# Feature-map attention and two MoE blocks on one core: weights' exponents rebased by ScalarE, a square kept in PSUM, the first loads from SP

## The chip, the cores and the metric

One core of a Trainium2 chip runs the whole program. The metric is device time in microseconds of one execution. Three runs of the kernel before took 1725.16, 1725.84 and 1729.33 us (median 1725.84). TensorE (PE in the rows, PEld for its weight loads), VectorE (DVE), ScalarE (ACT), GpSimd (POOL) and the queue engine SyncE (SP) each work through their own instructions in order.

## The reference

```python
def phi(x):                                  # x: (8, 8, 576, 64)
    proj = einsum('bhsd,df->bhsf', x, w_phi)             # 64 -> 128
    proj = proj - max(abs(proj), axis=-1, keepdims=True)
    return concatenate([exp(proj), exp(-proj)], axis=-1)
q_p, k_p = phi(q), phi(k)
kv = einsum('bhsf,bhsd->bhfd', k_p, v)
z = sum(k_p, axis=2)
x = einsum('bhsf,bhfd->bhsd', q_p, kv) / (einsum('bhsf,bhf->bhs', q_p, z)[..., None] + 1e-06)
x = x.transpose(0, 2, 1, 3).reshape(4608, 512)
h = x @ w_in                                 # moe1: 512 -> 2048
x = (h - tanh(h)) @ w_out                    # 2048 -> 512
a, b = x @ w1, x @ w2                        # moe2: 512 -> 1024
out = (a * b @ w3) @ w_out2                  # 1024 -> 1024 -> 512
```

The MoE weights arrive as 64-bit floats and are turned into 32-bit ones on the chip; each is then used as a high and a low part, with three products (hh, lh, hl) for one.

## The kernel before, in words

**Attention** works on 32 steps of one pair of batches and one head, in tiles of 128 rows, nine to a step. The tiles are taken in slots of four (`G`), so nine slots make four steps. In a slot TensorE projects k and, a step later, q of the slot's tiles (`p_pe`), turns the q differences of the slot before (`t_pe`), adds up kv (`kv_pe`) and, in eight slots of nine, makes one half of an output (`o_pe`); in some it also sums z (`z_pe`) and turns kv (`kv_turn`). VectorE takes maximum and difference of every p (L227, L229) and copies kv and half of the outputs out of PSUM; ScalarE takes the exponentials; GpSimd sums k's features. An output goes from PSUM to a buffer `st` and from there in six stores by SP to DRAM. p has three PSUM banks (`ps_h`), which moe1's h uses later.

**Weight chunks** run beside it, 26 of 128x512 in attention (tiles `craw`, `ct`), 92 of 128x256 in moe1 (`eraw`, `et`). `conv_steps` reads the two 32-bit words of each 64-bit float: ScalarE takes Abs of the high word read as a float (L117), VectorE takes a maximum with 2^-15 (L121), shifts left by 3 and masks (L124), and sets the sign and top bit from the raw word (L127); ScalarE scales the low word (L132), GpSimd adds the two (L135), ScalarE rounds to the high part (L139) and GpSimd subtracts for the low part (L142, or L607 elsewhere).

**moe1** goes through 9 blocks of 512 rows times 16 chunks of w_in, 144 n. Each n has twelve products into h (`mm1`) and twelve into four y banks (`mm2`), which lags by two n. Between them stands `act_g`: u = h^2 and tanh on ScalarE (L515, L516), s = (u + C1)^2 and the mask m (L517, L518), h - tanh (L522), then on VectorE u = h C2 u (L523), u = (s + C0) u (L525) and a predicated copy for small h (L526). In `act_g(n)`, after m, the g of n - 1 is split: gh on ScalarE (L541), gl on GpSimd (L542). SBUF pools of moe1 lie where attention's lay, so the first write to a tile there waits for the last user of that place, stores from `st` included. The next block's x is loaded, multiplied by the reciprocal (L1029) and split (L1035, L1036) in between.

**moe2** follows with all its products in TensorE's order; the first two `w34` products are mixed with moe1's last `mm2`.

Order is set by the code: each engine executes what it is given in the order in which the loops call it.

Of the kernel before, what the change touches and what calls it, by code (L numbers as in the profile page):

```python
# [8 lines left out]
F32 = mybir.dt.float32  # L9
# [3 lines left out]
ACTF = mybir.ActivationFunctionType  # L13
ALU = mybir.AluOpType
# [24 lines left out]
CW = S // 2  # L39
CE = S // 4  # L40
# [5 lines left out]
C0 = 4.726447630264936  # L46


TINY = 2.0 ** -15
FC_EARLY = 13  # L50


# [1 line left out]
def kernel(ctx, tc, qk_in, v_in, w_phi, w_in, w_out, w12, w3t_in, wo2, out):  # L54
    nc = tc.nc
    PE, ACT, DVE, POOL, SP = nc.tensor, nc.scalar, nc.vector, nc.gpsimd, nc.sync
    PSUM = bass.MemoryType.PSUM
# [45 lines left out]
    def words(raw, dt=U32):  # L103
        r = raw.bitcast(dt).rearrange("p (n two) -> p n two", two=2)
        return r[:, :, 0], r[:, :, 1]

    def conv_steps(pool, pre, n, load, dst, nb=1, nraw=None):

        o = {}

        def s_load():
            o["raw"] = pool.tile([128, n], I64, tag=f"{pre}raw", name=f"{pre}raw", bufs=nraw)
            load(o["raw"])

        def s_abs():
            o["t"] = pool.tile([128, n], U32, tag=f"{pre}t", name=f"{pre}t", bufs=nb)
            ACT.activation(o["t"].bitcast(F32), words(o["raw"], F32)[1], ACTF.Abs)  # L117

        def s_max():
            t = o["t"].bitcast(F32)  # L120
            DVE.tensor_scalar(t, t, TINY, None, ALU.max)  # L121

        def s_shift():
            DVE.tensor_scalar(o["t"], o["t"], 3, 0x3FFFFFF8, ALU.logical_shift_left, ALU.bitwise_and)  # L124

        def s_a():
            DVE.scalar_tensor_tensor(o["t"], words(o["raw"])[1], 0xC0000000, o["t"], ALU.bitwise_and, ALU.bitwise_or)  # L127

        def s_c():

            o["c"] = words(o["raw"])[0]
            ACT.activation(o["c"], words(o["raw"])[0], ACTF.Copy, scale=2.0 ** -29)  # L132

        def s_add():
            POOL.tensor_tensor(o["t"], o["t"], o["c"], ALU.add)  # L135

        def s_hi():
            o["hi"], o["lo"] = dst()
            ACT.activation(o["hi"], o["t"].bitcast(F32), ACTF.Copy)  # L139

        def s_lo():
            POOL.tensor_tensor(o["lo"], o["t"].bitcast(F32), o["hi"].bitcast(F32), ALU.subtract)  # L142

        on_act.update((s_abs, s_c, s_hi))
        return [s_load], [s_abs], [s_max, s_shift], [s_c, s_a], [s_add], [s_hi], [s_lo], lambda: o["t"].bitcast(F32)

    def fc_view(t):
        return t.rearrange("p k f -> p (k f)")

    def w_in_chunk(pool, i, part=0, of=1, pre="c", nb=1, nraw=None):  # L150
        nk = NK // of
        c = slice(part * nk * 128, (part + 1) * nk * 128)

        def dst():
            if part == 0:
                slots["in", i] = two("wi", i, [NK, 128])
            return tuple(fc_view(t[:, part * nk:(part + 1) * nk]) for t in slots["in", i])

        return conv_steps(pool, pre, DM // of, lambda raw: SP.dma_start(raw, w_in[i][:, c]), dst, nb, nraw)

    def w_out_chunk(pool, i, part=0, of=1, pre="c", nb=1, nraw=None):
        c = slice(part * DM // of, (part + 1) * DM // of)

        def dst():
            if part == 0:
                slots["out", i] = two("wo", i, [DM])
            return tuple(t[:, c] for t in slots["out", i])

        return conv_steps(pool, pre, DM // of, lambda raw: SP.dma_start(raw, w_out[i * 128:(i + 1) * 128, c]), dst, nb, nraw)
# [2 lines left out]

    def attention():
        with ExitStack() as es:
            pool = es.enter_context(tc.tile_pool(name="att", bufs=2))
            one = es.enter_context(tc.tile_pool(name="att1", bufs=1))
            ps_t = es.enter_context(tc.tile_pool(name="ps_t", bufs=1, space=PSUM))
# [13 lines left out]

            qk, vv = {}, {}

            def load_step(st):
                t = qk[st] = pool.tile([128, PT], F32, tag="qk", name="qk")
                if st == 0:
                    for c in (slice(0, 512), slice(512, PT)):
                        SP.dma_start(t[64:, c], qk_in[st][64:, c])
                elif st == NPAIR:
                    ACT.dma_start(t[:64], qk_in[st][:64])  # L200
                else:
                    ACT.dma_start(t, qk_in[st])

            def load_v(st):
                if st < NPAIR:
                    vv[st] = pool.tile([128, TPP + 1, D], F32, tag="v", name="v", bufs=3)
                    ACT.dma_start(vv[st], v_in[st])

            pq, pk, dq, dk, kp, pt, qp = {}, {}, {}, {}, {}, {}, {}

# [160 lines left out]

            def o_out(st, c, ps):
                bp, h = divmod(st - 1, H)
                t = pool.tile([128, CW + CE], F32, tag="st", name="st")
                if c:
                    DVE.tensor_copy(t, ps[:, :CW + CE])
                else:
                    ACT.activation(t, ps[:, :CW + CE], ACTF.Copy)
                for b in range(2):
                    c0 = bp * PT + b * S + c * CW  # L380
                    SP.dma_start(num_d[h * D:(h + 1) * D, c0:c0 + CW], t[b * D:(b + 1) * D, :CW])
                    for e in range(2):
                        r = 64 * b + 32 * e
                        SP.dma_start(den_d[bp, h:h + 1, c0 - bp * PT + e * CE:c0 - bp * PT + (e + 1) * CE], t[r:r + 1, CW:])
                return bp if c and h == H - 1 else None
# [25 lines left out]
            for i in (1, 0):  # L411
                SP.dma_start(wphi[i * D:(i + 1) * D], w_phi)
            for st in range(2):
                load_step(st)
                load_v(st)
            DVE.memset(ones, 1.0)
            o_at = {}
            for st in range(1, n_steps):
# [6 lines left out]
            for s in range(n_end):  # L425
# [40 lines left out]
                for n in tiles_of(s - 1) if ok(s - 1) else ():  # L466
                    st, t = where(n)
                    if t == TPP - 1 and st + 2 < n_steps:
                        load_v(st + 2)
                for n in tiles_of(s) if ok(s) else ():  # L470
                    st, t = where(n)
# [28 lines left out]
    def moe1():  # L500
        with ExitStack() as es:
            p1 = es.enter_context(tc.tile_pool(name="m1", bufs=1))
            p2 = es.enter_context(tc.tile_pool(name="m2", bufs=2))
            p3 = es.enter_context(tc.tile_pool(name="m3", bufs=2))
            ps_y = es.enter_context(tc.tile_pool(name="ps_y", bufs=1, space=PSUM))

            gg, yy, tt = {}, {}, {}

            def act_g(n, ys):
                h = hh[n]  # L510
                u = p2.tile([128, 512], F32, tag="u", name="u")
                s = p1.tile([128, 512], F32, tag="s", name="s")
                t = p2.tile([128, 512], F32, tag="t", name="t")
                m = p1.tile([128, 512], F32, tag="m", name="m")
                ACT.activation(u, h, ACTF.Square)  # L515
                ACT.activation(t, h, ACTF.Tanh)  # L516
                ACT.activation(s, u, ACTF.Square, bias=c1_sb)  # L517
                ACT.activation(m, u, ACTF.Relu, bias=lim_sb, scale=-1.0)  # L518
                g_parts(n - 1)
                for d in range(3):  # L520
                    y_out(ys, d)
                DVE.tensor_tensor(t, h, t, ALU.subtract)  # L522
                DVE.scalar_tensor_tensor(u, h, C2, u, ALU.mult, ALU.mult)  # L523
                y_out(ys, 3)
                DVE.scalar_tensor_tensor(u, s, C0, u, ALU.add, ALU.mult)  # L525
                DVE.copy_predicated(t, m.bitcast(U32), u)  # L526

                x = extra.get(n, [])
                for f in x:
                    if f in on_act:  # L530
                        f()
                del hh[n]
                tt[n] = t

            def g_parts(n):
                if n < 0:
                    return
                t = tt.pop(n)
                gh = p3.tile([128, 512], F32R, tag="gh", name="gh")
                gl = p3.tile([128, 512], F32R, tag="gl", name="gl")  # L540
                ACT.activation(gh, t, ACTF.Copy)  # L541
                POOL.tensor_tensor(gl, t, gh.bitcast(F32), ALU.subtract)  # L542
                gg[n] = gh, gl

            def y_out(ys, d):
                if ys is None:
                    return
                j, pss = ys
                if d == 3 and j == NB - 1:
                    t = p2.tile([128, 512], F32, tag="t", name="t")  # L550
                else:
                    t = p1.tile([128, 512], F32, tag="yo", name="yo", bufs=3)
                if d < 3:
                    ACT.activation(t, pss[d], ACTF.Copy)
                else:
                    DVE.tensor_copy(t, pss[d])
                (ACT if d < 3 else SP).dma_start(y_d[d * 128:(d + 1) * 128, j * 512:(j + 1) * 512], t)
# [117 lines left out]
            for i in range(FC_EARLY, NFC):  # L675
                for f in (w_in_chunk, w_out_chunk):
                    for part in range(2):
                        c = f(p2, i, part, 2, "e", 5, 3)
# [8 lines left out]
            for n in range(n_all + LAG):  # L687
# [5 lines left out]
                if n == n_all:  # L693
                    g_parts(n - 1)
# [398 lines left out]
```

## Time and profile before

| | before |
|---|---|
| median of 3 runs | 1725.84 us |
| the profiled execution's own time | 1728.21 us |
| its span, first to last instruction | 1726.4 us |
| TensorE busy (modelled ends) | 1693.6 us, 98% |
| VectorE, ScalarE, GpSimd busy | 1352.1, 926.0, 1014.1 us |
| mean granted TensorE clock | 0.998 |

The profile is of one execution. Busy time is the sum of an engine's instructions; an instruction that waits for a resource after it has started counts as busy. The span has three stages: attention to 351 us, moe1 to about 1149, then moe2, in which TensorE and its weight loads are busy without a gap.

### The profile page before, as it was taken

How to read it: one execution, taken by the hardware profiler on the slowest of the kernel's cores; microseconds unless marked ns; L12 is line 12 of the kernel's file. 1: busy time of each engine (PE TensorE's matmuls, PEld its weight loads, DVE VectorE, ACT ScalarE, POOL GpSimd, SP SyncE). 2: the span in 40 equal slices, each digit the busy share in tenths (PEclk: the TensorE clock that was granted, in tenths of full speed). 3: DMA queues.
4: the chain of work that ended last, by engine and by line, in shares of the span. 5: the costliest groups of instructions: out<-in, count | busy, mean ns of one | idle time of the engine just before them, and what ended most of it. 6: DMA issues, size and time to landing. Idle time of an engine off the chain costs nothing.

```text
span 1726.4 us, 30481 instructions
## 1 busy us (share of the span) xinstructions
PE 1693.6 (98%) x10640; PEld 1436.0 (83%) x10640; DVE 1352.1 (78%) x1910; ACT 926.0 (54%) x1881; POOL 1014.1 (59%) x966
## 2 busy tenths in 40 slices
PE   7999999999999999999999999999999999999999
PEld 5666666668877888878888788888999999999999
DVE  6999999769887888888999897755757666666664
ACT  4666676557666666767777676534322232322221
POOL 5787888737576767675767575234525253535341
PEclk9999999999999999999999999999999999999999
DMA  5555555322223332333434332728988898889885
GB/s 165 158 162 164 179 176 176 96 75 76 83 95 116 110 133 93 117 106 120 126 116 125 116 111 89 263 64 294 320 283 296 282 297 278 301 274 305 277 265 197
DMA packets 173113, 305.57 MB, mean 177 GB/s; under 512 B 21728, under 2 KB 57952, under 8 KB 172960
## 3 DMA queue, kind: packets, MB, share of 16 engines
q1 hardware_dynamic: 159920, 267.48, 47.6%
q10 hardware_dynamic: 13040, 36.15, 6.6%
q8 instruction: 84, 1.38, 0.3%
q14 instruction: 69, 0.57, 0.1%
HBM read 240.34 MB, written 63.21 MB: 176 GB/s over the span
## 4 chain that ended last, share of the span: by engine, by line
PE 72%; DVE 15%; DMA 5%; ACT 2%; POOL 2%; issue 2%; SPq 2%; DVEq 0%; ACTq 0%; POOLq 0%
PE h L495 16%; PE y L571 15%; PE q L826 14%; PE q L835 7%; PE pa L826 6%; PE o L835 3%; DVE u L525 3%; PE h L733 3%; DVE t L526 2%; PE p L220 2%; PE kv L298 2%; PE o L355 2%; DVE m L227 2%; DVE et L124 1%; DMA num_d<-st 1%
## 5 line engine op out<-in xcount | busy, mean ns | idle before, releaser
L542 POOL TENSOR_TENSOR gl<-t,gh 128x512 fp32r<-128x512 f32 x144 | 201.7, 1401 | 177.2 <-ACT gh L541 118.5
L571 PE MATMUL y<-gh,w 128*128 128x512 f32 x936 | 237.4, 391 | 4.4 <-ACT gh L541 2.7
L826 PE MATMUL q<-w,w 128*128 128x384 f32 x1152 | 215.1, 334 | 0.0
L571 PEld LDWEIGHTS y<-gh,w 128*128 128x128 f32 x936 | 176.0, 188 | 42.4 <-ACT gh L541 3.4
L525 DVE SCALAR_TENSOR_TENSOR u<-s,u 128x512 f32<-128x512 f32 x144 | 202.3, 1405 | 4.7
L826 PEld LDWEIGHTS q<-w,w 128*128 128x128 f32 x1152 | 201.0, 188 | 0.0
L897 POOL TENSOR_TENSOR xa<-c,c 128x384 f32<-128x384 f32 x48 | 51.9, 1082 | 249.8 <-DVE c L896 179.3
L495 PE MATMUL h<-xa,w 128*128 128x512 f32 x780 | 188.2, 391 | 0.0
L515 ACT ACTIVATE u<-h 128x512 f32<-128x512 f32 x144 | 85.8, 596 | 183.5 <-PE h L495 177.0
L495 PEld LDWEIGHTS h<-xa,w 128*128 128x128 f32 x780 | 147.2, 189 | 31.2 <-issue 0.2
L526 DVE COPY_PREDICATED t<-m,u 128x512 f32<-128x512 uint32 x144 | 165.7, 1151 | 5.0
L876 ACT ACTIVATE c<-pa 128x384 f32<-128x384 f32 x48 | 23.6, 493 | 237.5 <-PE pa L826 190.9
L495 PE MATMUL h<-xb,w 128*128 128x512 f32 x624 | 150.0, 389 | 0.0
L571 PE MATMUL y<-gl,w 128*128 128x512 f32 x468 | 132.6, 396 | 6.9 <-POOL gl L542 6.7
L495 PEld LDWEIGHTS h<-xb,w 128*128 128x128 f32 x624 | 117.1, 188 | 24.5
L135 POOL TENSOR_TENSOR et<-et,eraw 128x256 uint32<-128x256 uint32 x92 | 68.8, 748 | 111.9 <-ACT u L515 35.8
L240 ACT ACTIVATE kp<-dk 128x512 f32<-128x512 f32 x144 | 83.0, 627 | 86.5 <-DVE dk L229 80.6
L522 DVE TENSOR_TENSOR t<-h,t 128x512 f32<-128x512 f32 x144 | 98.3, 683 | 39.5 <-ACT t L516 39.4
L523 DVE SCALAR_TENSOR_TENSOR u<-h,u 128x512 f32<-128x512 f32 x144 | 98.6, 685 | 34.0 <-ACT m L518 33.7
L227 DVE TENSOR_REDUCE m<-p 128x4 f32<-128x512 f32 (+1 forms) x145 | 98.4, 679 | 28.6 <-PE p L220 28.4
L835 PE MATMUL q<-w,w 128*128 128x384 f32 x612 | 112.8, 334 | 0.0
L571 PEld LDWEIGHTS y<-gl,w 128*128 128x128 f32 x468 | 87.4, 189 | 30.5 <-POOL gl L542 12.8
(156 smaller groups left out, 3870.1 us busy)
## 6 DMA issues: line engine op xcount, KB each, us to landing
w<-w_d SPq DMA_DIRECT2D x504, 256.0 KB
w_d<-w SPq DMA_DIRECT2D x84, 256.0 KB
qk<-in_qk ACTq DMA_DIRECT2D x31, 576.0 KB
v<-in_v ACTq DMA_DIRECT2D x32, 320.0 KB
num_d<-st SPq DMA_DIRECT2D x128, 72.0 KB
xn<-num_d SPq DMA_DIRECT2D x36, 256.0 KB
xb<-y_d SPq DMA_DIRECT2D x24, 384.0 KB
eraw<-in_w SPq DMA_DIRECT2D x32, 256.0 KB
```

Source lines behind the costliest of these rows:

```text
L227: DVE.tensor_reduce(m[:, :n], what[g][:, j], AX.X, ALU.max, apply_absolute_value=True)
L240: ACT.activation(kp[g][:, sgn, span(js)], dk[g][:, span(js)], ACTF.Exp, scale=1.0 - 2 * sgn)
L495: PE.matmul(ps, a[:, kk, :], b[kk], start=m == 0, stop=m == 3 * NK - 1)
L515: ACT.activation(u, h, ACTF.Square)
L522: DVE.tensor_tensor(t, h, t, ALU.subtract)
L523: DVE.scalar_tensor_tensor(u, h, C2, u, ALU.mult, ALU.mult)
L525: DVE.scalar_tensor_tensor(u, s, C0, u, ALU.add, ALU.mult)
L526: DVE.copy_predicated(t, m.bitcast(U32), u)
L542: POOL.tensor_tensor(gl, t, gh.bitcast(F32), ALU.subtract)
L571: PE.matmul(yy[j][d], w[:, d * 128:(d + 1) * 128], x, start=i == 0 and m == 0, stop=i == NFC - 1 and m == 2,)
L826: PE.matmul(ps, w[:, a, c], x[b][:, kk, :], start=start and m == 0, stop=m == 5, skip_group_check=True)
L835: PE.matmul(ps, w[:, a, c], x[:, b, :], start=start and kk == 0 and n == 0, stop=kk == 3 and n == 2, skip_group_check=True,)
```

## The change

The Abs of the weights' high word gets a scale of 2^-112, which moves the exponent to where the shift by 3 leaves nothing to clamp or mask; the maximum goes, and the shift has one operation. `st` gets a pool of its own, opened before attention's others. The first two steps' loads go through SP's queue. s is allotted in PSUM, in a bank that nothing used in moe1. The g of n = 0 is split at the end of `act_g(0)`.

```diff
-TINY = 2.0 ** -15
+REBASE = 2.0 ** -112
@@ conv_steps
-            ACT.activation(o["t"].bitcast(F32), words(o["raw"], F32)[1], ACTF.Abs)
-
-        def s_max():
-            t = o["t"].bitcast(F32)
-            DVE.tensor_scalar(t, t, TINY, None, ALU.max)
+            ACT.activation(o["t"].bitcast(F32), words(o["raw"], F32)[1], ACTF.Abs, scale=REBASE)
 
         def s_shift():
-            DVE.tensor_scalar(o["t"], o["t"], 3, 0x3FFFFFF8, ALU.logical_shift_left, ALU.bitwise_and)
+            DVE.tensor_scalar(o["t"], o["t"], 3, None, ALU.logical_shift_left)
 
         def s_a():
-            DVE.scalar_tensor_tensor(o["t"], words(o["raw"])[1], 0xC0000000, o["t"], ALU.bitwise_and, ALU.bitwise_or)
+            DVE.scalar_tensor_tensor(o["t"], words(o["raw"])[1], 0x80000000, o["t"], ALU.bitwise_and, ALU.bitwise_or)
...
-        return [s_load], [s_abs], [s_max, s_shift], [s_c, s_a], [s_add], [s_hi], [s_lo], lambda: o["t"].bitcast(F32)
+        return [s_load], [s_abs], [s_shift], [s_c, s_a], [s_add], [s_hi], [s_lo], lambda: o["t"].bitcast(F32)
@@ attention
+            outs = es.enter_context(tc.tile_pool(name="att0", bufs=2))
             pool = es.enter_context(tc.tile_pool(name="att", bufs=2))
...
-            def load_step(st):
+            def load_step(st, eng=ACT):
...
-                t = pool.tile([128, CW + CE], F32, tag="st", name="st")
+                t = outs.tile([128, CW + CE], F32, tag="st", name="st")
...
             for st in range(2):
-                load_step(st)
-                load_v(st)
+                load_step(st, SP)
+                load_v(st, SP)
@@ moe1
+            ps_g = es.enter_context(tc.tile_pool(name="ps_g", bufs=1, space=PSUM))
...
-                s = p1.tile([128, 512], F32, tag="s", name="s")
+                s = ps_g.tile([128, 512], F32, tag="s", name="s")
...
                 tt[n] = t
+                if n == 0:
+                    g_parts(0)
 
             def g_parts(n):
-                if n < 0:
+                if n not in tt:
                     return
```

In the changed program's rows line numbers differ by up to 4; the names stay.

On SP the program begins with these rows; `craw` are the weight chunks. Before:

```order
L412 DMA wphi<-in_w_phi 64x128 x2
L198 DMA qk<-in_qk 64x512
L198 DMA qk<-in_qk 64x640
L159 DMA craw<-in_w_in 128x512
L169 DMA craw<-in_w_out 128x512
```

And now:

```order
L409 DMA wphi<-in_w_phi 64x128 x2
L195 DMA qk<-in_qk 64x512
L195 DMA qk<-in_qk 64x640
L204 DMA v<-in_v 128x640
L199 DMA qk<-in_qk 128x1152
L204 DMA v<-in_v 128x640
L155 DMA craw<-in_w_in 128x512
L165 DMA craw<-in_w_out 128x512
```

Three loads have come in from ScalarE's queue, where they were the first instructions behind the table load, and stand ahead of the first chunks.

On VectorE a chunk (`ct`) stands between the maxima and differences of two slots. Before:

```order
L229 TENSOR_TENSOR dq<-p,m 128x512
L121 TENSOR_SCALAR ct<-ct 128x512
L124 TENSOR_SCALAR ct<-ct 128x512
L227 TENSOR_REDUCE m<-p 128x4
L229 TENSOR_TENSOR dk<-p,m 128x512
```

And now:

```order
L226 TENSOR_TENSOR dq<-p,m 128x512
L120 TENSOR_SCALAR ct<-ct 128x512
L224 TENSOR_REDUCE m<-p 128x4
L226 TENSOR_TENSOR dk<-p,m 128x512
```

One instruction of 128x512 has gone at each of 26 such places, and one of 128x256 at 92 places in moe1.

On ScalarE, where moe1 begins (the brackets name what an instruction waits for: PE, DVE, Activation, Pool, or a DMA semaphore). Before:

```order
L515 ACTIVATE u<-h 128x512 [waits DMAHW2_49,DMAHW3_49,DMAHW1_49,DMAHW4_49,DMAHW0_49,DMAHW5_49,DVE_49,DMAHW6_49,PE_49,DMAHW7_49,Activation_49,Pool_49]
L516 ACTIVATE t<-h 128x512
L517 ACTIVATE s<-u,cs 128x512 [waits Activation_49]
L518 ACTIVATE m<-u,cs 128x512
L515 ACTIVATE u<-h 128x512 [waits PE_49]
L516 ACTIVATE t<-h 128x512
L517 ACTIVATE s<-u,cs 128x512 [waits DVE_49,Activation_49]
L518 ACTIVATE m<-u,cs 128x512 [waits DVE_49]
L541 ACTIVATE gh<-t 128x512
```

And now:

```order
L513 ACTIVATE u<-h 128x512 [waits PE_49,DVE_49,Activation_49,Pool_49]
L514 ACTIVATE t<-h 128x512
L515 ACTIVATE s<-u,cs 128x512 [waits DVE_49,Activation_49]
L516 ACTIVATE m<-u,cs 128x512
L541 ACTIVATE gh<-t 128x512 [waits DVE_49]
L513 ACTIVATE u<-h 128x512 [waits PE_49]
L514 ACTIVATE t<-h 128x512
L515 ACTIVATE s<-u,cs 128x512 [waits Activation_49]
L516 ACTIVATE m<-u,cs 128x512
```

The first u no longer waits for any DMA, and gh of n = 0 has moved from behind the second m to behind the first, where it waits for VectorE.

## Rows read from the trace of the kernel before

**Rows 1.** Chain of waits, 322 to 331 us: start us, us, what.

```profile
322.23 1.45 PE kv L298 x12
...
325.27 0.22 PE kv L332 x8
...
326.58 0.59 PE tr L261 x4
327.17 0.33 PE kv L341 x3
327.50 1.01 PE kv L298 x8
328.51 0.97 PE o L355 x8
329.48 0.63 PE o L364 x16
330.11 1.09 PE p L220 x16
```

**Rows 2.** Six windows of nine slots, summed: us, busy of PE, PEld, DVE, ACT, POOL.

```profile
sum 250.58, PE 244.70 PEld 165.98 DVE 230.95 ACT 167.17 POOL 207.55; mean PE 40.78 PEld 27.66 DVE 38.49 ACT 27.86 POOL 34.59
```

**Rows 3.** Chain of waits, the first pieces of the program.

```profile
1.99 6.00 DMA qk<-in_qk
...
8.12 5.60 PE p L220 x29
```

**Rows 4.** Window 2 to 8 us: busy per engine, clock, DMA share, GB/s.

```profile
2.00:8.00 6.00, 0.00 (x0) 0.00 (x0) 0.00 (x0) 0.22 (x2) 0.00 (x0) 1.00 0.96 286
```

**Rows 5.** Groups by line, VectorE, attention: xcount | busy us, mean ns | idle before.

```profile
L124 DVE TENSOR_SCALAR ct<-ct 128x512 uint32<-128x512 uint32 x26 | 22.8, 877 | 0.9
L121 DVE TENSOR_SCALAR ct<-ct 128x512 f32<-128x512 f32 x26 | 20.2, 777 | 0.0
```

**Rows 6.** Chain of waits where moe1 begins.

```profile
355.44 1.14 DMA den_d<-st
...
356.68 0.60 ACT u L515
...
363.96 4.15 PE y L571 x10
368.10 2.73 PE h L495 x12
```

**Rows 7.** Timeline, TensorE: moe1's first products, and the first of w34.

```profile
351.40 8.48 PE L495 MATMUL h<-xa,w 128*128 128x512 f32 x36
...
1149.23 5.60 PE L733 MATMUL h<-w 128*128 128x512 f32 x24
```

**Rows 8.** Windows of 2 us behind TensorE's two longest gaps; the clock follows the counts.

```profile
364.00:366.00 2.00, 2.00 (x6) 1.56 (x7) 1.97 (x2) 1.25 (x2) 1.59 (x1) 0.58 0.00 0
...
552.00:554.00 2.00, 2.00 (x6) 1.51 (x6) 1.05 (x2) 2.00 (x4) 2.00 (x4) 0.51 0.00 1
```

**Rows 9.** TensorE's waits, 351 to 1165 us: us in total, times, longest.

```profile
PE y L571 <- POOL gl L542: 6.7, 9, 1.9
...
PE y L571 <- DVE yo L556: 1.7, 1, 1.7
```

**Rows 10.** Timeline, VectorE and GpSimd, 359 to 364 us.

```profile
359.75 0.69 DVE L525 SCALAR_TENSOR_TENSOR u<-s,u 128x512 f32<-128x512 f32 x1
360.47 0.74 DVE L526 COPY_PREDICATED t<-m,u 128x512 f32<-128x512 uint32 x1
...
362.62 1.28 POOL L542 TENSOR_TENSOR gl<-t,gh 128x512 fp32r<-128x512 f32 x1 [23.16 <-DMA xn<-rden_d]
...
362.73 1.72 DVE L525 SCALAR_TENSOR_TENSOR u<-s,u 128x512 f32<-128x512 f32 x1
```

**Rows 11.** Groups by line, VectorE, moe1.

```profile
L525 DVE SCALAR_TENSOR_TENSOR u<-s,u 128x512 f32<-128x512 f32 x144 | 202.3, 1405 | 4.7
...
L523 DVE SCALAR_TENSOR_TENSOR u<-h,u 128x512 f32<-128x512 f32 x144 | 98.6, 685 | 34.0 <-ACT m L518 33.7
```

More of the change, by code (lines that the diff above doesn't have):

```diff
@@ L197, in load_step, with load_v @@
                     for c in (slice(0, 512), slice(512, PT)):
-                        SP.dma_start(t[64:, c], qk_in[st][64:, c])
+                        eng.dma_start(t[64:, c], qk_in[st][64:, c])
                 elif st == NPAIR:
-                    ACT.dma_start(t[:64], qk_in[st][:64])
+                    eng.dma_start(t[:64], qk_in[st][:64])
                 else:
-                    ACT.dma_start(t, qk_in[st])
-            def load_v(st):
+                    eng.dma_start(t, qk_in[st])
+            def load_v(st, eng=ACT):
                 if st < NPAIR:
                     vv[st] = pool.tile([128, TPP + 1, D], F32, tag="v", name="v", bufs=3)
-                    ACT.dma_start(vv[st], v_in[st])
+                    eng.dma_start(vv[st], v_in[st])
             pq, pk, dq, dk, kp, pt, qp = {}, {}, {}, {}, {}, {}, {}
```

## The prediction, made before the changed kernel ran

> **What bounds the kernel now.** I read the page's table of slices first (TensorE 98% busy, but its ends are modelled, so that says little), then the stages one by one: the chain of waits for TensorE's pace where nothing holds it, windows for what the same work really took, the groups by line for the other engines' durations, and the order of the two programs for what moves.
>
> *Attention (to 351 us).* The chain runs on TensorE alone for 19 us near the end of the stage and gives the price of each piece [rows 1]: in every slot p 1.09 and tr 0.59, kv 1.01 (1.45 where it has twelve records), one output half 0.97 + 0.63 in eight slots of nine, z 0.22 and the turn 0.33 four times in nine. Nine slots: 9 x 1.68 + 7 x 1.01 + 2 x 1.45 + 8 x 1.60 + 4 x 0.55 = 40.1 us. Six such stretches took 250.58 us, 41.76 each, with VectorE busy 230.95 [rows 2]. So TensorE is within 4% of its own floor, and loses 1.67 us per nine slots, to VectorE, which at 92% busy has nearly no slack. From 17 to 340 us there are 7.7 such stretches: 12.9 us in all that a lighter VectorE could give back, no more.
>
> *The start.* The first matmul comes at 8.12, behind q/k of step 0, whose load SP issues at 1.99 [rows 3].
>
> *moe1.* One mm1 or one mm2 is 2.72 us at full pace [rows 6]. From the first mm1 (351.40) to the first w34 (1149.23) [rows 7] lie 144 mm1 and 142 mm2, 286 x 2.72 = 777.9 us of 797.8: 19.9 us are lost. 5.8 of them lie before 368.10, where four of these should have taken 10.9 us and took 16.7: ScalarE's u waited until the last den_d store had landed (356.57), gl(0) started only at 362.62 [rows 10], and y then took 4.15 for ten records [rows 6] at a granted clock of 0.58, which is the 1.2 GHz level for most of the stretch, after TensorE had been idle [rows 8]. The other 14.1 lie at waits for gl (nine with the first, 6.7 us, the longest 1.9) and one for yo (1.7) [rows 9]; those rows count only open idle time, the rest is pipelining lost around them, delays too short to be listed, and one more stretch at the low clock behind the longest wait [rows 8].
>
> moe2 after that is gapless on TensorE, and nothing in it changes. So 36 to 37 us are to be had at most: 3 to 4, 12.9, 5.8, 14.1.
>
> **The change part by part.**
>
> *First pairs from SP.* The same bytes move; v of step 0 and all of step 1 now stand behind q/k of step 0 instead of sharing the 16 engines with it from another queue. Before, the stretch from 2 to 8 us moved 286 GB/s [rows 4], and that first load took 6.0 us. Alone behind wphi it has 0.2 MB to wait for, 0.7 us at that rate; its issue ends near 2.6, and a small store needs 1.14 us from its issue to its landing [rows 6], so it lands between 4.2 and 5.2. I take 5.0: 3.0 us won, between 0 (if something else needed holds p) and 3.9. Step 1 is needed after sixteen p records, at the start's 0.19 us each [rows 3], 3 us later; its 1.25 MB (with all ahead of it) at that rate, from 2 us on and with the same landing time, are there by about 7.5, just in time. The weight chunks queue behind three more issues of SP (1 to 2 us), and are first used at slot 2, hidden by the 5.6 us of p. The Trainium skill, SBUF — State Buffer, section "Door 1: The DMA port swizzle", speaks against the size: data for partitions 64 to 127 alone, as this load is, reach half of the SBUF ports. By that the 0.7 us would double and the term would be 2.3; no row here isolates it.
>
> *max and mask gone.* 26 chunks in attention lose L121, 0.777 us, 20.2 us in all; L124 stays at 0.877 [rows 5]. Both are longer than the work in them: L124 stands right behind L121 and finds GpSimd's next instruction in its way. Alone it will wait about as L121 does now. So a chunk saves between 0.42 (the shortest L121) and 0.9 us; I take 0.8, 2.8 us per nine slots (3.4 chunks). VectorE's share of the 40.1 us floor goes from 38.5 to 35.7, from 96% to 89%. It is still bursty (copies, a chunk and the reciprocals meet in some slots), so I count 9 of the 12.9 us won, with 4 and 12.9 as ends. ACT's Abs gains a constant scale in the same instruction: 0, since ScalarE is idle a third of the time here.
>
> *st in its own pool.* The st buffers no longer lie under u but under xb, whose first write comes two n later. u, t and the first eraw lose the wait for stores; SP still issues the stores back to back to about 355, but no engine on the path waits for them. u can start when h is done, 2.8 us after 351.40, at 354.3 instead of 356.7: 2.4 us.
>
> *First g at once.* Before, gh(0) stood behind the four ScalarE passes of n = 1; now it waits on VectorE for L526 of n = 0, and u to m of n = 1 queue behind it. From u to the end of L526 took 4.5 us [rows 6, 10], so gh, one ScalarE pass of 0.6 like u [rows 6], is done at 359.5 and gl, 1.28, at 360.8. TensorE has three mm1 until 359.6 and needs gl 0.45 later: 0.8 us idle, where before it stood from 359.6 to 362.6, and I take it that the clock then stays up. n = 1 is delayed by 2.3 us on ScalarE: its gh comes at 365.0, wanted at 365.3. Won together with st: 4.5 of 5.8, between 2 and 5.5.
>
> *s into PSUM.* L525 takes 0.69 while GpSimd is idle and 1.72 when gl runs beside it, ending just after gl [rows 10]; its mean is 1.405. L523, with the same size and one input in PSUM, has 0.685 throughout [rows 11]. No row has ScalarE writing PSUM, nor L525 with an input there: bounds 0.69 and 1.405, and I take 0.69 by L523. This frees 0.72 x 144 = 103 us of VectorE, none of it on TensorE's path while gl is in time. What counts is the burst: L127 of the next chunk starts 0.7 earlier, so does GpSimd's queue behind it, and GpSimd's sums no longer wait for L525. The listed gl are late by 1.9 at most; I move them up by 0.7 to 1.2, which removes all but two or three: 8.5 of 14.1, between 3 and 11; the yo stall (1.7) stays. The max that goes here too, 92 times, points the same way. What speaks against is a rule of the Trainium skill, SBUF — State Buffer, section "SBUF: two separate sides": VectorE with two SBUF inputs and GpSimd exclude each other for whole instructions. The trace agrees (1.72 against 0.69), and it has a second side: L526 now comes up while gl still runs, and waits there instead, up to 0.5 us each time, so that of the 103 us only some 60 to 80 would be seen on VectorE. The sum on TensorE stays as it is, since gl is then no later.
>
> Sum: 3.0 + 9 + 4.5 + 8.5 = 25.0 us. The profiled execution took 1728.2 (span 1726.4 and 1.8 around it): 1703.2. The median of the runs, 1725.84, is 2.4 lower than that execution, so the forecast for the runs is 1701.
>
> **Rivals.**
>
> 1. *TensorE's waits are in the bursts, not in VectorE's mean.* The recips, the empty slots and GpSimd's queue still make it wait; attention gives 4, moe1 3, the ends 6: 13 us, 1713. For it: GpSimd is over 80% busy in attention [rows 2], and gl's lateness is a GpSimd queue. Against: the stalls in attention come in slots with a chunk.
>
> 2. *All waits go.* 36 us, 1690. Against it: 89% on a bursty VectorE, and yo.
>
> 3. *The change doesn't do what it says.* The single shift waits for GpSimd as long as both did, and L525 stays at 1.4 because what holds it is not where s lies. Then only the loads, st and the first g count: 7.5 us, 1718. For it: L124 keeps its time; against: L523.
>
> 4. *Slower: traffic in the eighth PSUM bank holds TensorE's accumulation.* Per n one write (0.72) and one read (0.69) come on; if TensorE stood still for all of it, 1.41 x 144 = 203 us. It decides from 25 / 144 = 0.17 us per n; at a quarter of the overlap, 0.35, the time is 1726 - 25 + 51 = 1752. Against it: four reads of h per n (two by each engine) already stand beside mm1 and mm2, which keep 2.72. For it only that no row has such a write.
>
> **How the numbers follow.** Forecast (gain 17 to 32) 0.69; rival 1 0.13; rival 2 0.07; rival 3 0.05; rival 4 0.03; 0.03 left for smaller losses that just cancel. Range 1692 to 1714: below it lies most of rival 2, above it rivals 3 and 4 and a part of 1. A measurement of this kernel tells about 0.3%, 5.2 us, from no change. Faster: forecast, rivals 1, 2 and 3, less the corner of 3 that gives under 5.2 us: 0.93; slower 0.03; within 0.04.
>
> **What would show it.** First matmul near 5.0 (right: 4.2 to 5.5). Nine slots in 40.4 to 40.9. One ct instruction per chunk between ScalarE's Abs and L127's successor, at 0.5 to 0.9 us. TensorE idle under 1 us before y(0), clock 1.00 there. L525's successor at 0.69 whatever GpSimd does, L526's longer than 1.15. At most three waits of y on gl. It is wrong if nine slots stay at 41.7 with VectorE under 90%, or if mm1 and mm2 are longer than 2.72 in stretches without a wait.

## The result, and the profile after

| | before | after |
|---|---|---|
| median of 5 runs | 1725.87 us (1725.16 to 1729.33) | 1702.06 us (1699.87 to 1703.66) |
| the profiled execution, its span | 1728.21, 1726.4 us | 1701.24, 1699.5 us |
| VectorE, GpSimd busy | 1352.1, 1014.1 us | 1190.1, 993.5 us |

The ratio is 0.9856, interval 0.9841 to 0.987: 23.8 us won by the medians. The two profiled executions differ by 27.0, since that of before lies 2.3 us above its median and that of after 0.8 below. By stage they split as follows (all times from the two traces):

| stretch | before | after | won |
|---|---|---|---|
| to the first transpose | 16.92 | 13.38 | 3.5 |
| first transpose to first mm1 | 334.5 | 326.0 | 8.5 |
| first three mm1 and first y | 16.70 | 12.42 | 4.3 |
| from there to the first w34 | 781.1 | 770.6 | 10.5 |
| moe2 | 577.2 | 577.1 | 0 |

**The start.** The timeline of TensorE in the profile after (start us, us, line, tiles, count; in brackets the idle time before and what ended it), which answers to [rows 3]:

```profile
4.66 6.06 PE L217 MATMUL p<-wphi,qk 64*128 64x128 f32 x30 [4.66 <-DMA qk<-in_qk]
...
13.38 0.55 PE L258 MATMUL tr<-ident,dq 128*128 128x128 f32 x3
...
19.77 0.66 PE L258 MATMUL tr<-ident,dq 128*128 128x128 f32 x4 [0.25 <-ACT qp L279]
...
24.55 0.65 PE L258 MATMUL tr<-ident,dq 128*128 128x128 f32 x4 [1.14 <-ACT qp L279]
```

The load that it waits for, in the chain of waits (start us, us, what), took 6.00 us in [rows 3] and now takes:

```profile
1.99 2.53 DMA qk<-in_qk
```

The first matmul comes 3.46 us earlier. The distances between transposes are the slots; those that begin at 16.10 and 19.77 take 3.67 and 4.78, though they hold no output and need about 3 (3.05 and 3.02 in better, where the first chunks come three slots later). The first weight chunk comes to VectorE at 14.8 us, just ahead of them.

**Attention.** Six windows of nine slots, summed (answers to [rows 2]); TensorE's waits in this stage (in total, times, longest), first one row of before, then after; and one wait of after in the timeline:

```profile
sum 244.09, PE 242.26 PEld 165.44 DVE 213.76 ACT 167.01 POOL 203.86; mean PE 40.38 PEld 27.57 DVE 35.63 ACT 27.83 POOL 33.98
```

```profile
PE kv L341 <- DVE kvs L328: 5.2, 10, 1.2
```

```profile
PE tr L258 <- ACT qp L279: 2.0, 3, 1.1
PE kv L338 <- DVE kvs L325: 1.0, 2, 0.7
```

```profile
136.55 0.72 PE L217 MATMUL p<-wphi,qk 64*128 64x128 f32 x8 [0.85 <-DMA qk<-in_qk]
```

Nine slots take 40.68 us instead of 41.76, against a floor of 40.1; VectorE does 17 us less in the six stretches. The wait for a load of q/k at 136.55 is new: none of the three executions with the old loads has one in this stage.

**Where moe1 begins.** The chain of waits (answers to [rows 6]), and a window on TensorE's idle time there (columns as in [rows 8]):

```profile
342.54 0.07 ACT u L513
...
346.33 0.76 DVE t L524
...
347.11 0.64 ACT gh L541
...
347.88 1.29 POOL gl L542
...
349.21 2.56 PE y L571 x10
351.77 2.27 PE h L492 x10
```

```profile
348.00:350.00 2.00, 1.32 (x5) 0.76 (x5) 0.72 (x2) 2.00 (x5) 1.16 (x1) 1.00 0.83 261
```

The first u starts as soon as h is there and no store stands in the chain. gh follows VectorE's last instruction (t L524) at once, gl follows gh, and TensorE waits 0.68 for it. Its clock stays at 1.00, so the ten y take 2.56 where they took 4.15.

**moe1.** The groups of VectorE by line (answers to [rows 5, 11]), and TensorE's waits from 330 to 1165 us (to [rows 9]):

```profile
L524 DVE COPY_PREDICATED t<-m,u 128x512 f32<-128x512 uint32 x144 | 160.4, 1114 | 4.9
L521 DVE SCALAR_TENSOR_TENSOR u<-h,u 128x512 f32<-128x512 f32 x144 | 99.6, 692 | 69.6 <-ACT m L516 69.5
L523 DVE SCALAR_TENSOR_TENSOR u<-s,u 128x512 f32<-128x512 f32 x144 | 99.5, 691 | 4.6
...
L123 DVE SCALAR_TENSOR_TENSOR et<-eraw,et 128x256 uint32<-128x256 uint32 x92 | 71.2, 774 | 0.0
...
L120 DVE TENSOR_SCALAR ct<-ct 128x512 uint32<-128x512 uint32 x26 | 19.8, 761 | 0.0
```

```profile
PE y L571 <- POOL gl L542: 2.3, 3, 1.2
PE y L571 <- DVE yo L556: 0.5, 1, 0.5
```

Where nothing is late, the chain of waits shows the pace of mm2 and mm1:

```profile
359.93 2.72 PE y L571 x12
362.65 2.72 PE h L492 x12
```

u = (s + C0) u, with s in PSUM, takes 691 ns instead of 1405 (680 to 693 over all 144), the same as its neighbour L521 with h in PSUM. Of nine waits for gl three are left, one of them the first of moe1 above. The chunk's one shift takes 761 ns where two instructions took 777 and 877. Counted as in the prediction, 286 products of 2.72 us, moe1 loses 5.1 us of 783.1 where it lost 19.9.

### The profile page after: what moved, and what is told of

Read it like the earlier page. It is cut to its first block, busy times and chain, and to the rows that moved or that the text cites. A ratio compares the mean times of both kernels' runs of the same rounds, so it can differ in the third digit from the quotient of the medians.

```text
span 1699.5 us, 30356 instructions
## 1 busy us (share of the span) xinstructions
PE 1683.9 (99%) x10640; PEld 1434.1 (84%) x10640; DVE 1190.1 (70%) x1792; ACT 921.3 (54%) x1881; POOL 993.5 (58%) x966
## 4 chain that ended last, share of the span: by engine, by line
PE 94%; DVE 2%; ACT 1%; DMA 1%; POOL 1%; issue 1%; ACTq 0%; SPq 0%; DVEq 0%; POOLq 0%
PE y L571 22%; PE h L492 22%; PE q L826 15%; PE q L835 7%; PE pa L826 6%; PE p L217 4%; PE kv L295 4%; PE o L352 3%; PE o L835 3%; PE h L733 3%; PE o L361 2%; PE tr L258 2%; PE kv L338 1%; DMA qk<-in_qk 1%; DMA y_d<-yo 0%
## 5 line engine op out<-in xcount | busy, mean ns | idle before, releaser
L542 POOL TENSOR_TENSOR gl<-t,gh 128x512 fp32r<-128x512 f32 x144 | 194.2, 1348 | 225.5 <-ACT gh L541 162.9
L826 PEld LDWEIGHTS q<-w,w 128*128 128x128 f32 x1152 | 201.1, 188 | 0.0
L524 DVE COPY_PREDICATED t<-m,u 128x512 f32<-128x512 uint32 x144 | 160.4, 1114 | 4.9
L521 DVE SCALAR_TENSOR_TENSOR u<-h,u 128x512 f32<-128x512 f32 x144 | 99.6, 692 | 69.6 <-ACT m L516 69.5
L835 PEld LDWEIGHTS q<-w,w 128*128 128x128 f32 x612 | 106.7, 188 | 0.0
```

The costliest lines, as they stand in the source:

```text
L826: PE.matmul(ps, w[:, a, c], x[b][:, kk, :], start=start and m == 0, stop=m == 5, skip_group_check=True)
L835: PE.matmul(ps, w[:, a, c], x[:, b, :], start=start and kk == 0 and n == 0, stop=kk == 3 and n == 2, skip_group_check=True,)
```

## The experiments

Each was made from the changed kernel, except s_alone; all times are medians of 4 or 5 runs. "After" in the comparisons is the 1702.06 above. The kernel before ran again beside each group of experiments, each group on a chip of its own, and came out at 1726.54, 1726.96 and 1725.30 instead of 1725.87. So each cost can be had in two ways, from 1702.06, or from how much less than 23.8 us the kernel then wins over the runs of before beside it:

| part taken back | from 1702.06 | against before beside it |
|---|---|---|
| s in SBUF (s_back) | 8.0 | 7.3 |
| maximum in attention (max_att) | 8.7 | 8.1 |
| maximum in moe1 (max_moe) | 0.8 | 0.1 |
| three loads (loads_back) | 1.2 | 0.6 |
| late g (g_late) | 0.4 | -0.7 |
| st (st_back) | 2.9 | 1.8 |

The interval of the change itself is 2.5 us to either side, so only the first two are clear of the noise by their times; the others are read from the traces.

### s back in SBUF (s_back)

```diff
-            ps_g = es.enter_context(tc.tile_pool(name="ps_g", bufs=1, space=PSUM))
-                s = ps_g.tile([128, 512], F32, tag="s", name="s")
+                s = p1.tile([128, 512], F32, tag="s", name="s")
```

> The changed kernel with s back in SBUF, all else as changed. Theory: in moe1 the gain of 10.5 us behind the transition is that the second u on VectorE no longer waits for GpSimd, so it mostly goes: moe1 7 to 10 us longer than in the changed kernel, some 1710; that instruction back at about 1.4 us, gl late five times or more. Rival: what helped moe1 was the lighter weight chunk on VectorE (one instruction less for 92 chunks); then s_back loses under 3 us, 1702 to 1705.

Measured: 1710.06 us (1709.02 to 1711.13), 8.0 above after. First the VectorE groups, then TensorE's waits over the same stretch as above:

```profile
L522 DVE SCALAR_TENSOR_TENSOR u<-s,u 128x512 f32<-128x512 f32 x144 | 208.5, 1448 | 4.6
...
L123 DVE SCALAR_TENSOR_TENSOR et<-eraw,et 128x256 uint32<-128x256 uint32 x92 | 55.7, 605 | 0.0
```

```profile
PE y L570 <- POOL gl L541: 6.5, 7, 1.6
```

This line alone brings back the long u and four of the waits for gl; attention keeps its pace (six windows 244.36). From the first mm1 to the first w34 moe1 loses 12.9 us beyond 2.72 a product, against 5.1 in after. The theory held, not its rival. VectorE's whole busy time is 1295.7 against 1190.1: 105.6 us go with s, of which TensorE sees about 8.

### s in PSUM, nothing else (s_alone)

```diff
# on the kernel before
+            ps_g = es.enter_context(tc.tile_pool(name="ps_g", bufs=1, space=PSUM))
-                s = p1.tile([128, 512], F32, tag="s", name="s")
+                s = ps_g.tile([128, 512], F32, tag="s", name="s")
```

> The kernel before with s in PSUM and nothing else. Theory: moe1 gains 7 to 8 us as it loses them when s goes back, attention and the first y as before, some 1718.5. Rival: with the maximum still in the chunks VectorE has no slack for it to use, or the two gains are the same gain: under 4 us, 1722 or more.

Measured: 1717.23 us (1715.95 to 1718.85), ratio 0.9948 (0.9935 to 0.996), 9.7 under the runs of before on the same chip (1726.96). So s is worth 7 to 10 us whether it goes first or last, and it doesn't need the lighter chunk: the rival fell. The timeline of TensorE shows where the other parts are missing, and a window behind it the clock (columns as in [rows 8]):

```profile
363.07 0.73 PE L572 MATMUL y<-gh,w 128*128 128x512 f32 x2 [2.67 <-ACT gh L542]
364.49 0.50 PE L572 MATMUL y<-gl,w 128*128 128x512 f32 x1 [0.68 <-POOL gl L543]
...
366.77 1.05 PE L572 MATMUL y<-gh,w 128*128 128x512 f32 x2
```

```profile
366.00:368.00 2.00, 2.00 (x6) 1.58 (x5) 1.93 (x5) 1.98 (x5) 1.29 (x2) 0.50 0.00 0
```

TensorE stood 2.67 and 0.68 us, and then the clock fell to its 1.2 GHz level (0.50 in the window): two products take 1.05 where at full clock they take 0.62.

### One more maximum in attention (max_att)

```diff
         def s_shift():
+            if pre == "c":
+                DVE.tensor_scalar(o["t"].bitcast(F32), o["t"].bitcast(F32), 2.0 ** -126, None, ALU.max)
```

> The changed kernel with one more VectorE maximum per weight chunk, in attention's 26 chunks only. Theory: attention's 8.5 us came from VectorE's time, so 7 to 9 us return, nine slots at 41.5 us again, some 1710; moe1 unchanged. Rival: attention gained because the slots stand otherwise to the transfers since the earlier start; then under 3 us return, 1702 to 1705.

Measured: 1710.79 us (1710.42 to 1711.62), 8.7 above after; first mm1 at 348.18, 8.8 later; counted from the first transpose, which came 0.8 later in this execution, 8.0. moe1 takes 784.1 us, 783.1 in after. Six windows of nine slots and TensorE's longest waits:

```profile
sum 250.62, PE 244.74 PEld 165.99 DVE 230.97 ACT 167.12 POOL 207.58; mean PE 40.79 PEld 27.67 DVE 38.50 ACT 27.85 POOL 34.60
```

```profile
PE kv L340 <- DVE kvs L327: 5.2, 10, 1.2
```

26 instructions of VectorE give the sum of before again [rows 2], to 0.04 us, VectorE's busy time to 0.02, and the ten waits for kvs. So the maximum is what attention won behind the first transpose, to within half a microsecond. The mask, which did not come back here, is worth nothing that shows.

### One more maximum in moe1 (max_moe)

The same edit with `pre == "e"`, 92 instructions.

> The changed kernel with one more VectorE maximum per weight chunk, in moe1's 92 chunks only. Theory: VectorE has slack there once s lies in PSUM, so 0 to 3 us, 1702 to 1705. Rival (the chunk is what made gl late): 5 to 9 us, 1707 to 1711. Attention unchanged under both.

Measured: 1702.87 us (1701.25 to 1703.23); moe1 loses 5.8 us beyond 2.72 a product, after 5.1 and the same kernel once more (after_again) 6.5: nothing that can be told apart. The theory held. The groups of VectorE:

```profile
L122 DVE TENSOR_SCALAR et<-et 128x256 uint32<-128x256 uint32 x92 | 66.3, 721 | 3.2
L121 DVE TENSOR_SCALAR et<-et 128x256 f32<-128x256 f32 x92 | 31.5, 343 | 0.0
```

With the maximum ahead of it the shift takes 721 ns, alone it takes 342 (after). The two groups take 66 us more than the one, VectorE's whole busy time is 56 us longer (1246.0), and TensorE does not see it.

### Three of the first loads back on ScalarE's queue (loads_back)

```diff
-                load_step(st, SP)
-                load_v(st, SP)
+                load_step(st, SP if st == 0 else ACT)
+                load_v(st)
```

> The changed kernel with the loads of v of step 0 and of step 1 issued by ScalarE again. Theory: the first matmul is back at about 8.1 us and all after it moves by the same 3.5 us, 1705.5. Rival: the later start is made up behind it, since VectorE or the next loads set the first slots; first matmul at 8.1, but the first mm1 under 1.5 us later, 1702 to 1703.5.

Measured: 1703.28 us (1703.09 to 1704.11), 1.2 above after or 0.6, which is not clear of noise. It fits the rival; the theory's 1705.5 lies above every run. The start of TensorE's timeline:

```profile
7.18 5.46 PE L217 MATMUL p<-wphi,qk 64*128 64x128 f32 x30 [7.18 <-DMA qk<-in_qk]
...
15.81 0.55 PE L258 MATMUL tr<-ident,dq 128*128 128x128 f32 x3
```

The first matmul is 2.52 us later than in after, the first transpose 2.43, the first mm1 (340.74) only 1.39. Two places in after account for the difference of 1.04: its wait of 0.85 for q/k at 136.55, which doesn't stand here, and the two slots with the first chunk, 0.37 longer than here. But max_moe and s_back, with the loads of after, have their first mm1 at 340.64 and 340.86, no earlier than here. In max_moe step 1 was late itself:

```profile
10.26 1.65 PE L219 MATMUL p<-wphi,qk 64*128 64x128 f32 x12 [1.35 <-DMA qk<-in_qk]
```

That wait stands in two of the nine executions with the new loads (1.35, and 1.44 in st_back).

### g of n = 0 late again (g_late)

```diff
-                if n == 0:
-                    g_parts(0)
```

> The changed kernel with the g of n = 0 split behind the ScalarE passes of n = 1 again. Theory of the prediction: the early split was worth what is left of 4.5 us after st, 2.1 us at the first y, 1704. Rival, read from the changed kernel's trace: gh(0) waits there for VectorE until 347.1, and behind the passes of n = 1 it would come at about 347.8, so only 0.7 us; 1702.5 to 1703, and n = 1 earlier on ScalarE.

Measured: 1702.49 us (1701.62 to 1703.59), no difference from after, as the rival said. TensorE's timeline, and ScalarE's row of gh in after:

```profile
338.53 8.46 PE L492 MATMUL h<-xa,w 128*128 128x512 f32 x36
347.60 0.73 PE L569 MATMUL y<-gh,w 128*128 128x512 f32 x2 [0.62 <-ACT gh L539]
349.01 0.50 PE L569 MATMUL y<-gl,w 128*128 128x512 f32 x1 [0.68 <-POOL gl L540]
```

```profile
347.11 0.63 ACT L541 ACTIVATE gh<-t 128x512 fp32r<-128x512 f32 x1 [2.27 <-DVE t L524]
```

y comes 0.6 us later behind the first mm1 than in after, no more. gh(0) has to wait for VectorE's fourth instruction in any case (ScalarE stood idle for 2.27 us ahead of it in after); the four passes of n = 1 fit for the most part into that time.

### st in the pool of before (st_back)

```diff
-            outs = es.enter_context(tc.tile_pool(name="att0", bufs=2))
-                t = outs.tile([128, CW + CE], F32, tag="st", name="st")
+                t = pool.tile([128, CW + CE], F32, tag="st", name="st")
```

> The changed kernel with st in attention's pool again, over which moe1's u comes to lie. Theory: u waits for the last den_d store, about 2.5 us later than when h is done, gh and gl as much later; TensorE stands 2.5 to 3 us more before y(0), and the clock falls behind it: 3.5 to 4.5 us, 1705.5 to 1706.5. Rival: the early split hides a part of it and the clock stays up: 2.5 us or less, 1704.5.

Measured: 1704.97 us (1704.24 to 1707.23), 2.9 above after, 1.8 against the runs of before beside it. The chain where moe1 begins, TensorE's timeline there, and the window behind its idle time:

```profile
347.71 1.12 DMA den_d<-st
348.94 0.60 ACT u L512
```

```profile
354.17 0.73 PE L570 MATMUL y<-gh,w 128*128 128x512 f32 x2 [2.02 <-ACT gh L540]
355.58 0.50 PE L570 MATMUL y<-gl,w 128*128 128x512 f32 x1 [0.68 <-POOL gl L541]
```

```profile
356.00:358.00 2.00, 2.00 (x11) 1.63 (x10) 1.58 (x3) 1.76 (x5) 0.78 (x1) 1.00 0.00 0
```

u waits for the last store again, and TensorE for 2.02 us more than in after. With 2.02 and 0.68 us of idle time the clock stayed at 1.00; with 2.67 and 0.68 (s_alone) it did not. So the rival held: the theory's 3.5 to 4.5 us counted on the clock to fall. By the second reckoning the 2.02 us are the whole cost; the first leaves 0.9, which these rows do not show.

### Two versions that go further (better, better2, after_again)

The first two chunk slots lose 2.4 us in after, and the first y ends on gl's products alone, which costs a wait. `better` delays all chunks by three slots, puts twelve transposes ahead of the first p, and mixes gl's products into y(0):

```diff
-            step = (n_slots - 7) / len(chunks)
-                at = int(i * step)
+            step = (n_slots - 10) / len(chunks)
+                at = 3 + int(i * step)
+            for i in range(12):
+                PE.transpose(wt[:, i % 4 * 128:(i % 4 + 1) * 128], ident, ident)
-                if 0 < i < NFC - 1:
+                if n == 0 or 0 < i < NFC - 1:
```

> The changed kernel with three additions: twelve transposes of the identity while the first loads are on their way, so that TensorE is not cold at the first p; the first weight chunk three slots later; in the first y (n = 0) the products with gl last. Theory: p's first thirty records take 2 to 4 us instead of 6, but the load of step 1 then holds them, so 1 to 2 us at the first transpose; the slots behind it 1 to 2 us shorter without a chunk; 0.7 at the first y: 3 to 5 us in all, 1697 to 1699. Rival: the start is set by the loads alone and the chunk only moves its wait: under 1 us, 1701 to 1702.

Measured: 1700.59 us (1699.88 to 1703.1), not to be told from after. p's first thirty records still took 5.46 us behind 2.8 us of transposes, so these did nothing for them and that part of the theory fell. The two slots took 3.05 and 3.02, but what follows them took 1.5 us longer than in after, where chunks now stood closer, and the first mm1 came at 338.37, 1 us earlier.

`better2` leaves the transposes out, keeps the old spacing, and delays only the first ten chunks. It ran beside the changed kernel once more:

```diff
-                at = int(i * step)
+                at = max(int(i * step), int(3 + 2.3 * i))
-                if 0 < i < NFC - 1:
+                if n == 0 or 0 < i < NFC - 1:
```

> The changed kernel with two edits: the first weight chunks of attention begin three slots later and catch up with their old places within ten chunks, and the first y no longer ends on gl's products alone but mixes them as the middle ones do. Theory: what those places showed is won and not given back: about 2.4 us in the first two chunk slots (3.7 and 4.8 go to 3.1 each) and 0.9 in the first y (3.8 to 2.9), first mm1 near 337, in all 3 us under the changed kernel on the same chip, near 1699. Rival: the waits belong to VectorE's total load in the denser slots and only move, as where all chunks were shifted: first mm1 not before 338.3, 1 us or less in all, intervals overlapping.

> The changed kernel once more, for comparison on the same chip as the kernel beside it. Theory: 1702 us as before (1699.9 to 1703.7), first mm1 near 339.3, y(0) 3.8 us for ten records, first two slots that hold a chunk 3.7 and 4.8 us.

Measured: 1699.24 us (1697.84 to 1700.8) against 1701.80 (1700.69 to 1702.86) for the changed kernel on the same chip, 2.6 under it; ratios to before 0.9844 (0.983 to 0.9859) and 0.9857 (0.984 to 0.9873). These overlap, so the size is not settled, but TensorE's timeline shows it at the two places meant:

```profile
18.66 0.66 PE L258 MATMUL tr<-ident,dq 128*128 128x128 f32 x4
...
21.68 0.66 PE L258 MATMUL tr<-ident,dq 128*128 128x128 f32 x4
...
336.63 8.46 PE L492 MATMUL h<-xa,w 128*128 128x512 f32 x36
345.08 2.12 PE L571 MATMUL y<-gh,w 128*128 128x512 f32 x8
...
347.95 2.88 PE L492 MATMUL h<-xa,w 128*128 128x512 f32 x12
```

The second slot is 3.02 (21.68 less 18.66) instead of 4.78. The first mm1 comes at 336.63, after_again's at 339.62; 1.4 of these 3.0 us are an earlier first transpose (12.89 against 14.27), which the edit doesn't explain, and 1.6 lie behind it, so most of the 2.4 of the two slots stays won. y(0) takes 2.87 instead of 3.82 and waits for nothing. What each of the two edits is worth in the time was not measured by itself.

## Why the prediction was right, and where its terms were off

Forecast 1701, measured 1702.06. The sign, the range and the mechanism of the two large terms are as worked out. That the sum came within about 1 us is partly luck: the traces show 26.8 us where 25.0 were forecast, the medians 23.8, and the loads' term is not seen to reach the time. Rival 1, with 4 us in attention and 3 in moe1, and rival 2, with no wait left, fell with the two large terms.

**Attention, 9 forecast: right.** 8.5 by the trace, 8.0 to 8.7 by max_att alone. Nine slots take 40.68 (said: 40.4 to 40.9). That the floor of 40.1 was not reached is only in part for the reason named, bursts on VectorE: the waits listed in the six stretches are one of 0.71 for its copy kvs, at 264, and the one of 0.85 for a load; about 2 of the 3.5 us above the floor stand in no listed wait. The single shift at 0.76 lies inside 0.5 to 0.9, and about where L121 was, as said.

**s in PSUM, 8.5 forecast: right, on the low side.** 10.5 by the two traces, 7.3 to 8.0 by taking it back, 9.7 alone. u(s, u) is 0.69 whatever GpSimd does, three waits on gl are left (said: at most three), and the waits for yo stayed, as said (0.5 us here, 1.9 in after_again). With after_again's trace in place of this one the 10.5 would be 9.1. Rival 3, that where s lies does not matter, fell here; rival 4 too, since mm1 and mm2 keep 2.72 us with the eighth bank in use. The stated help from moe1's maximum fell: max_moe shows none.

**The step on the exclusion's second side failed.** The prediction said that L526's successor would wait instead, longer than 1.15, and that 60 to 80 of 103 us would be seen on VectorE. It took 1.114, less than in s_back (1.216). VectorE's busy time falls by 105.6 us where s goes last (s_back less after), though by 83.4 where it goes alone (before less s_alone). What got longer is another instruction, the sign setter of the next weight chunk, which reads two tiles in SBUF. These are its row, the shift's and L526's, before:

```profile
L526 DVE COPY_PREDICATED t<-m,u 128x512 f32<-128x512 uint32 x144 | 165.7, 1151 | 5.0
...
L124 DVE TENSOR_SCALAR et<-et 128x256 uint32<-128x256 uint32 x92 | 66.8, 727 | 3.2
L127 DVE SCALAR_TENSOR_TENSOR et<-eraw,et 128x256 uint32<-128x256 uint32 x92 | 49.1, 533 | 0.0
```

It went to 774 ns (605 in s_back), 15.5 us more than with s in SBUF. The chain of waits has it at one place, on the way to the wait for yo, 0.55 us at 963.83, so little was lost by it:

```profile
949.83 0.84 DVE et L123
```

The rule cited there from the Trainium skill, SBUF — State Buffer, section "SBUF: two separate sides", agrees with these rows: the instruction with an operand in PSUM is free of GpSimd (680 to 693 ns; 0.69 us at 704.73 too, where gl runs from 704.62 on), those with two in SBUF are not (1114 and 774 in the mean, 745 and 397 at the shortest). The step missed which of the latter comes next to GpSimd's instruction.

**st and the first g, 4.5 forecast: the sum right, the shares wrong.** 4.3 by the trace. The prediction gave st 2.4 and the early g the remaining 2.1. st_back gives 2.0 at TensorE's wait, g_late 0.6. The failed step is that gh stood behind four passes of n = 1: it took that delay as 2.3 us, but about three quarters of it lie in time in which gh waits for VectorE anyhow. What fills the gap between 2.0 + 0.6 and 4.3 is the clock: with either edit taken back alone TensorE stood idle 1.30 us (g_late) or 2.70 (st_back) and kept its speed; with neither in place it stood 3.35 (s_alone), and the clock fell to its 1.2 GHz level during the first y, as in before (4.15 us for ten records against 2.56). These 1.6 us belong to neither by itself.

**The loads, 3.0 forecast: right at the first matmul, not seen to reach the time.** The first matmul came at 4.66 (said: 4.2 to 5.5), 3.46 us earlier; over all executions it came at 4.66 to 4.95 with the new loads, at 7.18 to 8.81 with the old. By the estimate that the prediction took from the Trainium skill, SBUF — State Buffer, section "Door 1: The DMA port swizzle", the term would have been 2.3. The 3.46 lies above it, the 2.52 of loads_back near it, and no run isolates it, so this stays open. Taking three loads back costs 0.6 to 1.2 us, within the noise. "Just in time" was the failed step: step 1's q and k were late by 1.35 and 1.44 in two of nine executions, and in three a later load of q/k was, by 0.85 to 1.36 at 137 to 139 us, which no execution with the old loads shows. The first transposes stood at 15.81 to 17.79 with the old loads, and with those of after at 13.36 to 15.81: the start varies by over 2 us between executions, as much as the term itself.

Taken back one by one, the parts cost 22.0 us of the 23.8 by the first column of the table above and 17.2 by the second. The noise of six differences adds up in these sums, so they do not show whether anything is left over; what the clock adds where two edits are missing together is seen in the traces alone.

## What to carry to other kernels

The same instruction of VectorE can cost TensorE time in one stage and nothing in another: 26 maxima in attention were 8 to 9 us, a third of a microsecond each, 92 in moe1 none that showed, so price an edit by the stage and by the wait that ends last there. Two edits that each shorten one idle stretch of TensorE should be priced together, since the clock may hold with either and fall with neither. Work that only has to be done by some time can be moved out of the few slots where VectorE is late (better2); packed closer elsewhere it gave part of that back (better, one execution).

## What the runs showed of the hardware that was not expected

- p's first thirty records took 5.5 to 6.1 us in all executions that had no wait among them, 0.18 to 0.2 each at a granted clock of 1.00, where sixteen take 1.09 later [rows 1]. Twelve transposes ahead of them changed nothing. The row of the clock shows 1.00 also before the first matmul [rows 4], so it may tell nothing there. The cause stays open.
- An instruction of VectorE on one operand in SBUF, behind another of the same kind, pays more than the first: 727 against 355 ns for 128x256 in the kernel before, 721 against 343 in max_moe, 342 when it stands alone. That GpSimd's waiting instruction slips in between the two fits all three, and the trace of before has a case: the first at 700.46, GpSimd's L135 from 700.68 to 701.43, the second from 700.78 to 701.57. No run isolated it.
- ScalarE's pass that makes s took 695 ns in the mean with s in PSUM (after), 722 with s in SBUF (before).
